# Attention and gated MLP in one kernel: pair 2's queries in the mixed order, bias rows ahead of V, w_in behind a cast, and a new order of slots 4 and 7 to 9

## The chip, the cores and the metric

The kernel runs on one core of one Trainium2 chip. The metric is the device time of one execution in microseconds. The kernel before took 354.9 us, the median of three runs (354.85, 354.90 and 356.21); the profiled execution has a span of 352.8 us. TensorE's granted clock was 1.00 throughout.

## What is computed

Batch 8, 8 heads, 576 positions, head dimension 64; then an MLP on 4608 tokens of width 512 with 2048 hidden units. All inputs are float32.

```python
scores = 0.125 * q @ k.T                         # per batch and head, 576 x 576
cum    = cumsum(maximum(s, 0))                   # per batch and head
scores = where(key > query, -1e9, scores + minimum(-(cum_query - cum_key), 0))
x      = softmax(scores) @ v                     # heads side by side: 4608 x 512
h      = x @ w_in                                # 4608 x 2048
out    = (h * clip(h + 3, 0, 6) / 6) @ w_out     # 4608 x 512
```

## The kernel before

**Tiling.** Heads are taken two at a time: 32 pairs, four to a batch. The main loop `for p in range(NP)` has one slot for each pair. Scores are held with keys on partitions and queries along the row. A head has three groups of scores (`scores(p, hh, g)`, L400 and L415), each in one bank of PSUM; ScalarE takes exp into `P` (L434). The last 64 keys and queries of both heads are the corner (`corner(p)`, L472 and L480). `av` multiplies P by V (L499), V carrying a column of ones whose product is the softmax sum; `norm` divides by it on VectorE (L521, L522); `transpose_x` turns x on TensorE (L536) and copies it to `xT` (L541). The MLP works on blocks of 512 tokens: `m1` makes one 128-wide strip of h (L565), with ScalarE's `tr` (L580) and VectorE's `gT` (L581) behind it; `m2` makes a quarter of the sum for an output tile (L592). `m1_begin` starts an m1 with those of its four terms that are there.

**The bias.** The sum of s is an addition to the scores, and it comes in through four extra rows of the q and k operands: partitions 64 to 67 of the tile `qk`, which DMA copies from `rows_of` (`load_aug(p)`, L169). `rows_of` is computed once for 32 heads in the first microseconds.

**Queries in two orders.** q and k are loaded as f16 with several positions in a partition's row, and TensorE transposes them (L278; L265 for the mixed order). A copy from PSUM then brings positions in place. In the plain order it writes every sixth and second element (L322). In the mixed order, which `mixed(p, i)` chooses for the queries of pairs 3 to 6, 64 queries stand in groups of 16, and the copy writes runs of 16 (L310). A mixed pair uses a permuted causal mask (`shutm`), permuted bias rows (row 0 of `rows_of`, made on GpSimd by the cast at L850), and a permutation instead of the identity in `transpose_x`.

**Masks.** Pairs 0 to 3 add the mask of the diagonal with a matmul (L389, L459); from pair 4 GpSimd sets the masked part of P to zero after exp (`shut_out`, L444), and `av` waits for that.

**Order of the work.** Every engine runs its instructions in the order in which the program records them[...]. GpSimd issues the loads of q, k, w_in (1 MB at a time) and w_out, casts V from f32 (`cast_v`, L218 and L219) and cuts P. SyncE issues the loads of V (`load_v`, three transfers to a pair, two raw buffers in turn), most bias rows and the output. Each of the two queues has eight completion semaphores in turn, so an issue also waits for the transfer eight issues before it. Which half of the MLP a `group()` call records is written out in `plan`, one character a call: 1 an m1, 2 an m2, a point nothing. In PSUM, scores have two banks from slot 4 on, `ph` two, `po` two, the transposed q or k one (`t`), so every one of them waits for the reader of the bank's last contents.

**Around the change.** Until slot 3 the MLP has nothing to do. Slot 4 (`p == PPB`) is the first with m1. Its part before:

```python
            m1_begin(0, 0, NKC - 1)
            scores(p, 0, 1)
            transpose_x(p - 1)
            scores(p, 0, 2)
            m1_begin(0, 1, NKC - 1)
            pt = transpose_in(p + 1, 0)
            transpose_out(p + 1, 0, pt, pars=(0,))
            group()
            transpose_out(p + 1, 0, pt, pars=(1,))
            group()
```

There the two query copies stand between the groups, one ahead of each. Slots 6 to 9 have the same split.

Of the kernel before, what the change touches and what calls it, by code (L numbers as in the profile page):

```python
# [18 lines left out]
def kernel(  # L19
# [97 lines left out]
    def load_qk(p, i):  # L117
        b, h0 = p // PPB, 2 * (p % PPB)
        src = (q, k)[i][b, h0 : h0 + 2]
        if not flat(p):  # L120
            if not i:
                tok = work.tile([128, 24 * D], F16, tag="tok", bufs=4, name="tok")
                toks[p] = tok[0:96].rearrange("p (i h e d) -> p i h e d", i=2, h=2, e=6)
            if mixed(p, i):
                nc.gpsimd.dma_start(
                    out=toks[p][:, i]
                    .rearrange("p h e d -> p (h e d)")
                    .rearrange("p (t x) -> p t x", t=3),
                    in_=src.rearrange("h s d -> (h s) d").rearrange(
                        "(t p e) d -> p t (e d)", p=96, e=4  # L130
                    ),
                )
                return
            nc.gpsimd.dma_start(
                out=toks[p][:, i].rearrange("p h e d -> p h (e d)"),
                in_=src.rearrange("h (p e) d -> p h (e d)", e=6),
            )
        else:
            if p < NSW:
                if not i:  # L140
                    tok = work.tile([128, 24 * D], F16, tag="tok", bufs=4, name="tok")
                    toks[p] = tok[:, 0 : 18 * D]
                to, eng = toks[p], nc.gpsimd
            else:
                to, eng = raws[p % NRAW], nc.sync
            eng.dma_start(
                out=to.rearrange("p (i t d) -> p i t d", i=2, t=9)[:, i],
                in_=src.rearrange("h s d -> (h s) d").rearrange(
                    "(t p) d -> p t d", p=128
                ),  # L150
            )

    def load_v(p, eng):
        b, h0 = p // PPB, 2 * (p % PPB)
        vraw = vraws[p % NVRAW]
        for hh in range(2):
            eng.dma_start(
                out=vraw[:, hh, 0:4, :],
                in_=v[b, h0 + hh, 0:512, :].rearrange("(t p) d -> p t d", p=128),
            )  # L160
        eng.dma_start(
            out=vraw[0:64, :, 4, :],
            in_=v[b, h0 : h0 + 2, 512:SEQ, :].rearrange("h p d -> p h d"),
        )

    def load_aug(p, eng):
        for hh in range(2):
            g = 2 * p + hh
            eng.dma_start(  # L169
                out=qks[p % NQK][64:68, hh, :, 64 * hh : 64 * hh + SEQ],  # L170
                in_=rows_of[g // 32].rearrange("(r g) i t -> g r i t", g=32)[
                    g % 32, :, slice(0, 3, 2) if mixed(p, 0) else slice(1, 3), 0:SEQ
                ],
            )
# [6 lines left out]
    def load_w_in(c):  # L181
        nc.gpsimd.dma_start(
            out=w_in_sb[:, :, 512 * c : 512 * (c + 1)],
            in_=moe_w_in[:, 512 * c : 512 * (c + 1)].rearrange(
                "(kc p) f -> p kc f", p=128
            ),
        )
# [28 lines left out]
    def cast_v(p):  # L216
        vraw, va = vraws[p % NVRAW], vas[p % NVA]
        nc.gpsimd.tensor_copy(out=va[:, :, 0:4, 0:64], in_=vraw[:, :, 0:4, :])  # L218
        nc.gpsimd.tensor_copy(out=va[0:64, :, 4, 0:64], in_=vraw[0:64, :, 4, :])  # L219
# [63 lines left out]
        return pt  # L283

    def mixed(p, i):
        return i == 0 and PPB - 1 <= p < NPROD - 1

    def mix(ap):
        return ap.rearrange("p (g w v) -> p g w v", w=4, v=16)

    def unmix(ap):
        return ap.rearrange("p (g v w) -> p g w v", w=4, v=16)
# [292 lines left out]
    def m2(n, i):  # L585
# [31 lines left out]
    tail = [False]  # L617
    LAG = 12
    plan = list(
        "11.1.1."  # L620
        + "1.1.1.1."
        + "1.1.1.1."
        + "1.1.1212"
# [212 lines left out]
    head_out(0, 0, 1, pts[0], (A, V.tensor_copy))  # L836
    head_out(0, 1, 1, pts[1], (V.tensor_copy, V.tensor_copy))
    warm(NWARM[2])
    load_aug(1, nc.gpsimd)
    load_v(1, nc.sync)  # L840
    load_aug(2, nc.sync)
    load_stair(PPB, nc.sync)
    cast_v(0)
    for i in range(2):
        load_qk(3, i)
    load_v(2, nc.sync)
    cast_v(1)
    for i in range(2):
        load_qk(4, i)
    nc.gpsimd.tensor_copy(  # L850
        out=mix(rows_of[0][0:32, 0, 0:SEQ]), in_=unmix(C["c"][0:32])
    )


    I, U = load_w_in, load_w_out
# [1 line left out]
    for p in range(NP):  # L857
# [7 lines left out]
                    load_qk(p + 3, i)  # L865

        if p == 2:
            load_w_in(0)
            cast_v(2)
            qk_ahead()  # L870
            load_aug(5, nc.gpsimd)
        elif p == 3:
            cast_v(3)
            qk_ahead()
            load_aug(6, nc.gpsimd)
            load_w_in(1)
            cast_v(4)
        elif p >= PPB:
            qk_ahead()
            if NPE <= p + 2 < NP:  # L880
                if p + 2 >= NSW:
                    cast_qk(p + 2)
                crossbar_qk(p + 2)
# [25 lines left out]
        if p and p + 2 < NP:  # L909
            load_v(p + 2, nc.sync)  # L910
        if p == 1:
            load_aug(3, nc.sync)
            load_aug(4, nc.sync)
        if p == 2:
            for i in range(PPB + 1, NPROD):
# [15 lines left out]
        def get(i):  # L931
            if p + 1 < NPE:
                transpose(p + 1, i)
            elif nxt:
                spread(p + 1, i)
# [22 lines left out]
        if p == PPB:  # L958
            early[0] = False
            scores(p, 0, 0)  # L960
            pool_mid()
            av(p - 1, 1, 0)
            av(p - 1, 1, 1)
            norm(p - 1, 1)
            m1_begin(0, 0, NKC - 1)
            scores(p, 0, 1)
            transpose_x(p - 1)
            scores(p, 0, 2)
            m1_begin(0, 1, NKC - 1)
            pt = transpose_in(p + 1, 0)  # L970
            transpose_out(p + 1, 0, pt, pars=(0,))
            group()
            transpose_out(p + 1, 0, pt, pars=(1,))
            group()
        else:
            scores(p, 0, 0)
            pool_mid()
            if NPROD - 1 <= p + 1 < NPE:
                pt = transpose_in(p + 1, 0)
                transpose_out(p + 1, 0, pt, pars=(0,))  # L980
                group()
                transpose_out(p + 1, 0, pt, pars=(1,))
            else:
                get(0)
                group()
            scores(p, 0, 1)
            av(p - 1, 1, 0)
            if p >= NPE - 1:
                get(1)
            group()  # L990
            scores(p, 0, 2)
            av(p - 1, 1, 1)
            norm(p - 1, 1)
            group()
        if p == 12:
            cum2(whole)
        corner(p)
        if p == 11:
            new_sum()
            cum1(1, whole)  # L1000
# [1 line left out]
        if p > NPE:  # L1002
            x_done[0] = p - 1
        if p == PPB:
            get(1)
            av(p, 0, 0)
        scores(p, 1, 0)
        pool_end()
# [5 lines left out]
        scores(p, 1, 1)  # L1014
        if p != PPB:
            av(p, 0, 0)
        if PPB < p < NPROD:
            transpose_x(p - 1)
        elif p >= NPROD and p != 3 * PPB:
            crossbar_x(p - 1)  # L1020
# [53 lines left out]
```

## Time and profile before

| | busy us | share of span | instructions |
|---|---|---|---|
| TensorE matmul | 344.1 | 98% | 2914 |
| VectorE | 230.5 | 65% | 476 |
| ScalarE | 222.0 | 63% | 395 |
| GpSimd | 166.6 | 47% | 296 |

Busy shares are means over the whole span. By stages (busy us of TensorE, VectorE, ScalarE and GpSimd in each stretch, and what DMA moved):

| stretch, us | TensorE | VectorE | ScalarE | GpSimd | GB/s |
|---|---|---|---|---|---|
| 0 to 20 | 17.57 | 17.25 | 15.60 | 18.54 | 164 |
| 20 to 35 | 13.32 | 11.41 | 12.74 | 9.66 | 196 |
| 35 to 50 | 15.00 | 14.06 | 13.39 | 14.68 | 197 |
| 50 to 65 | 14.42 | 10.77 | 10.33 | 10.12 | 192 |
| 120 to 160 | 40.00 | 27.10 | 27.88 | 23.79 | 183 |
| 300 to 353 | 49.15 | 21.92 | 16.08 | 0.00 | 50 |

A share near the length of the stretch means that the engine hardly rests there. The end of a matmul in the records is modelled, and the next may start before it, so time lost on TensorE is best read from the distances between starts. Slots 0 to 3 end at about 26 us, slot 4 lasts from 26.1 to 34.7, slots 5, 6 and 7 begin at 34.7, 41.3 and 48.0.

### The profile page before, as it was taken

Reading aid. Unit: us, or ns where it says so; the run is one execution under the profiler, and the core shown is the slowest. Engines: PE = TensorE matmul, PEld = TensorE weight load, DVE = VectorE, ACT = ScalarE, POOL = GpSimd, SP = SyncE. Lnnn points to the kernel's source line nnn. Section 1 sums busy time; section 2 is a strip of 40 time slices with the busy share of each in tenths; the row PEclk is TensorE's granted clock in tenths of the full one; section 3 lists DMA queues with packets and bytes.
Section 4 is the critical chain, followed back from the end, with each engine's and each line's share of the span. In section 5 each row is a group of like instructions: output and inputs, shape, how many; then the busy total and the mean of one; then the engine's idle time right before and its main releaser. Section 6 shows DMA issues by size and latency. Waiting matters only on the chain.

```text
span 352.8 us, 7771 instructions
## 1 busy us (share of the span) xinstructions
PE 344.1 (98%) x2914; PEld 190.8 (54%) x2914; DVE 230.5 (65%) x476; ACT 222.0 (63%) x395; POOL 166.6 (47%) x296
## 2 busy tenths in 40 slices
PE   8998999999999999999999999999999999999995
PEld 3775666655555555555555555555555444444442
DVE  7996996686868677666666665767654544544531
ACT  6987895677787677666766666666665333444410
POOL 8976995676778556555555555555310000000000
PEclk9999999999999999999999999999999999999999
DMA  8999999999999999889898969796120101101112
GB/s 162 155 201 192 194 200 197 148 201 177 159 124 124 211 204 178 180 187 175 185 168 191 179 156 196 164 207 140 37 74 20 59 17 46 59 2 59 59 39 82
DMA packets 144616, 48.59 MB, mean 138 GB/s; under 512 B 130537, under 2 KB 139593, under 8 KB 144578
## 3 DMA queue, kind: packets, MB, share of 16 engines
q1 hardware_dynamic: 117138, 37.83, 53.4%
q0 software_dynamic: 27200, 9.97, 23.9%
q8 instruction: 23, 0.38, 0.5%
q10 hardware_dynamic: 240, 0.28, 0.2%
q14 instruction: 15, 0.12, 0.1%
HBM read 37.59 MB, written 9.44 MB: 133 GB/s over the span
## 4 chain that ended last, share of the span: by engine, by line
PE 85%; DMA 5%; DVE 5%; ACT 3%; issue 1%; POOL 0%; SPq 0%; ACTq 0%
PE po L592 34%; PE ph L565 32%; PE O L499 7%; PE S L415 6%; PE S L400 3%; DMA vraw<-in_v_dram 3%; DMA tok<-in_k_dram 1%; DVE qk L242 1%; DVE gT L581 1%; DVE qk L322 1%; PE pt L278 1%; ACT P L434 1%; ACT tr L580 1%; DMA s_all<-in_s_dram 1%; DVE x L522 1%
## 5 line engine op out<-in xcount | busy, mean ns | idle before, releaser
L581 DVE SCALAR_TENSOR_TENSOR gT<-tr,ph 128x512 f16<-128x512 f32 x144 | 98.7, 686 | 98.5 <-ACT tr L580 97.4
L565 PE MATMUL ph<-xT,w_in_sb 128*128 128x512 f16 x576 | 148.0, 378 | 0.8 <-DVE gT L581 0.6
L592 PE MATMUL po<-w_out_sb,gT 128*128 128x512 f16 x576 | 145.8, 379 | 0.0
L580 ACT ACTIVATE tr<-ph,bias 128x512 f32<-128x512 f32 x144 | 98.9, 687 | 73.3 <-PE ph L565 71.3
L434 ACT ACTIVATE P<-S 128x512 f16<-128x512 f32 x192 | 111.4, 595 | 39.4 <-PE S L400 22.3
L565 PEld LDWEIGHTS <-w_in_sb 128*128 128x128 f16 x576 | 51.3, 97 | 45.3 <-issue 1.1
L592 PEld LDWEIGHTS <-gT 128*128 128x128 f16 x576 | 50.1, 97 | 46.5 <-issue 0.2
L444 POOL TENSOR_SCALAR_AFFINE_SELECT P<-P 128x512 f16<-128x512 f16 x56 | 37.8, 674 | 46.9 <-ACT P L434 46.8
L415 PE MATMUL S<-qk 68*128 68x448 f16 (+3 forms) x256 | 49.0, 272 | 0.6 <-ACT P L434 0.6
L499 PE MATMUL O<-va,P 128*128 128x65 f16 x896 | 47.7, 193 | 0.0
L499 PEld LDWEIGHTS <-P 128*128 128x128 f16 x896 | 39.2, 97 | 13.5
L242 DVE COPY qk<-jt 64x768 f16<-64x768 f16 x84 | 37.4, 446 | 1.2
L415 PEld LDWEIGHTS <-qk 68*128 68x128 f16 x256 | 23.7, 98 | 24.2 <-issue 0.7
L522 DVE TENSOR_TENSOR x<-O,rl 128x320 f16<-128x320 f32 x64 | 31.4, 491 | 2.2
L169 POOL DMA_DIRECT2D qk<-rows_of x50 | 29.8, 598 | 2.2 <-PE S L400 1.6
L608 DVE TENSOR_SCALAR ob<-po 128x512 f32<-128x512 f32 (+1 forms) x36 | 24.3, 676 | 8.3 <-PE po L592 7.7
L444 POOL TENSOR_SCALAR_AFFINE_SELECT PC<-PC 128x128 f16<-128x128 f16 x28 | 8.5, 304 | 43.0 <-ACT PC L480 42.9
L400 PEld LDWEIGHTS <-qk 75*128 75x128 f16 (+1 forms) x256 | 18.8, 97 | 12.9 <-DVE qk L322 1.4
L400 PE MATMUL S<-qk 75*128 75x128 f16 (+1 forms) x256 | 24.8, 219 | 0.9 <-DVE qk L322 0.6
L218 POOL CAST va<-vraw 128x512 f16<-128x512 f32 x32 | 21.1, 659 | 2.8 <-DMA vraw<-in_v_dram 2.8
L322 DVE COPY qk<-pt 64x576 f16<-64x576 f16 x22 | 17.6, 805 | 4.6 <-ACT qk L322 4.1
L214 POOL CAST tok<-raw 128x576 f16<-128x576 f32 x28 | 18.0, 681 | 0.0
(77 smaller groups left out, 188.0 us busy)
## 6 DMA issues: line engine op xcount, KB each, us to landing
out_dram<-ob SPq DMA_DIRECT2D x35, 256.0 KB, 2.0
vraw<-in_v_dram SPq DMA_DIRECT2D x64, 128.0 KB, 4.7
raw<-in_q_dram SPq DMA_DIRECT2D x14, 288.0 KB, 3.6
raw<-in_k_dram SPq DMA_DIRECT2D x14, 288.0 KB, 4.2
tok<-in_q_dram POOLq DMA_DIRECT2D x18, 144.0 KB, 5.3
tok<-in_k_dram POOLq DMA_DIRECT2D x18, 144.0 KB, 6.5
w_in_sb<-in_moe_w_in_dram POOLq DMA_DIRECT2D x4, 512.0 KB, 7.3
w_out_sb<-in_moe_w_out_dram POOLq DMA_DIRECT2D x8, 256.0 KB, 9.1
```

The costliest lines, as they stand in the source:

```text
L169: eng.dma_start(out=qks[p % NQK][64:68, hh, :, 64 * hh : 64 * hh + SEQ], in_=rows_of[g // 32].rearrange("(r g) i t -> g r i t", g=32)[g % ...
L242: copies[par](out=qk[0:64, :, i, 128 * par : 128 * par + 256 * n].rearrange("p h (s two c) -> p h s two c", two=2, c=128)[:, :, :, 0, :], ...
L400: mm(S[:, c], lhsT=kT[rows, c], rhs=qT[rows, c], start=(j == 0 and not by_product), stop=(j == 3 and p >= NROW),)
L415: mm(S[:, c : c + w], lhsT=kT[0:68, 128 * j : 128 * (j + 1)], rhs=qT[0:68, 128 * (j + 1) : SEQ], start=(c == 0), stop=(c != 0 and p >= NROW),)
L434: nc.scalar.activation(out=pt[:, c], in_=S, func=AF.Exp, scale=0.125)
L444: nc.gpsimd.affine_select(out=part, in_=part, pattern=pattern, compare_op=ALU.is_ge, fill=0.0, base=0, channel_multiplier=-1,)
L499: mm(o[:, i, :], lhsT=lhsT, rhs=va[:, hh, j, 0:65], **kw)
L522: nc.vector.tensor_tensor(out=X[p][:, :, hh, :], in0=o[:, :, 0:64], in1=rl.to_broadcast([128, 5, 64]), op=ALU.mult,)
L565: mm(ph, lhsT=w_in_sb[:, kc, ft * 128 : (ft + 1) * 128], rhs=xT[:, kc, n * 512 : (n + 1) * 512], start=(kc == 0), stop=(kc == NKC - 1),)
L580: nc.scalar.activation(out=tr, in_=ph, func=AF.Relu, bias=bias3[:, 0:1])
L581: nc.vector.scalar_tensor_tensor(out=gTs[n][:, ft, :], in0=tr, scalar=6.0, in1=ph, op0=ALU.min, op1=ALU.mult)
L592: mm(po, lhsT=gTs[n][:, ft, t4 * 128 : (t4 + 1) * 128], rhs=w_out_sb[:, ft, :], start=(ft == 0), stop=(ft == NFT - 1),)
```

## The change

Four edits. The third pair's queries (pair 2) are mixed too, so that their copies write runs. The bias rows of pairs 1, 2 and 3 are issued on SyncE, those of pairs 2 and 3 ahead of pair 3's V, and the permuting cast on GpSimd, on which pair 2's rows now depend, comes earlier; the loads of pair 3's q and k go ahead of the first cast of V. The first load of w_in goes behind the cast of pair 2's V. In slot 4 the corner and both copies of the next queries come right behind the transposed x, ahead of the second `m1_begin`, the keys (`get(1)`) move behind the second head's second scores, and `plan` moves one m1 accordingly. In slots 7 to 9 the query copies are no longer split around `group()`; in slot 6 they still are. In the order of TensorE both programs have the same 5830 rows.

```diff
--- before.py
+++ after.py
@@ -283,7 +283,7 @@
         return pt
 
     def mixed(p, i):
-        return i == 0 and PPB - 1 <= p < NPROD - 1
+        return i == 0 and PPB - 2 <= p < NPROD - 1
 
     def mix(ap):
         return ap.rearrange("p (g w v) -> p g w v", w=4, v=16)
@@ -617,7 +617,7 @@
     tail = [False]
     LAG = 12
     plan = list(
-        "11.1.1."
+        "11..11."
         + "1.1.1.1."
         + "1.1.1.1."
         + "1.1.1212"
@@ -836,20 +836,21 @@
     head_out(0, 0, 1, pts[0], (A, V.tensor_copy))
     head_out(0, 1, 1, pts[1], (V.tensor_copy, V.tensor_copy))
     warm(NWARM[2])
-    load_aug(1, nc.gpsimd)
     load_v(1, nc.sync)
-    load_aug(2, nc.sync)
+    load_aug(1, nc.sync)
     load_stair(PPB, nc.sync)
-    cast_v(0)
     for i in range(2):
         load_qk(3, i)
+    cast_v(0)
     load_v(2, nc.sync)
+    nc.gpsimd.tensor_copy(
+        out=mix(rows_of[0][0:32, 0, 0:SEQ]), in_=unmix(C["c"][0:32])
+    )
+    load_aug(2, nc.sync)
+    load_aug(3, nc.sync)
     cast_v(1)
     for i in range(2):
         load_qk(4, i)
-    nc.gpsimd.tensor_copy(
-        out=mix(rows_of[0][0:32, 0, 0:SEQ]), in_=unmix(C["c"][0:32])
-    )
 
 
     I, U = load_w_in, load_w_out
@@ -865,8 +866,8 @@
                     load_qk(p + 3, i)
 
         if p == 2:
+            cast_v(2)
             load_w_in(0)
-            cast_v(2)
             qk_ahead()
             load_aug(5, nc.gpsimd)
         elif p == 3:
@@ -909,7 +910,6 @@
         if p and p + 2 < NP:
             load_v(p + 2, nc.sync)
         if p == 1:
-            load_aug(3, nc.sync)
             load_aug(4, nc.sync)
         if p == 2:
             for i in range(PPB + 1, NPROD):
@@ -966,16 +966,15 @@
             scores(p, 0, 1)
             transpose_x(p - 1)
             scores(p, 0, 2)
+            corner(p)
+            get(0)
             m1_begin(0, 1, NKC - 1)
-            pt = transpose_in(p + 1, 0)
-            transpose_out(p + 1, 0, pt, pars=(0,))
             group()
-            transpose_out(p + 1, 0, pt, pars=(1,))
             group()
         else:
             scores(p, 0, 0)
             pool_mid()
-            if NPROD - 1 <= p + 1 < NPE:
+            if p + 1 == NPROD - 1:
                 pt = transpose_in(p + 1, 0)
                 transpose_out(p + 1, 0, pt, pars=(0,))
                 group()
@@ -994,7 +993,8 @@
             group()
         if p == 12:
             cum2(whole)
-        corner(p)
+        if p != PPB:
+            corner(p)
         if p == 11:
             new_sum()
             cum1(1, whole)
@@ -1002,7 +1002,6 @@
         if p > NPE:
             x_done[0] = p - 1
         if p == PPB:
-            get(1)
             av(p, 0, 0)
         scores(p, 1, 0)
         pool_end()
@@ -1014,6 +1013,8 @@
         scores(p, 1, 1)
         if p != PPB:
             av(p, 0, 0)
+        else:
+            get(1)
         if PPB < p < NPROD:
             transpose_x(p - 1)
         elif p >= NPROD and p != 3 * PPB:
```

## The prediction

> **What bounds the kernel now.** I read the page first (busy shares, slices), then TensorE's instructions in order of time, then those of VectorE and GpSimd, then the chain that ended last, in the early window alone. Columns of the instruction views: start, duration, engine and line, operation, shape, count, and in brackets the engine's idle time before it and what ended it.
>
> ```profile
> PE 344.1 (98%) x2914; PEld 190.8 (54%) x2914; DVE 230.5 (65%) x476; ACT 222.0 (63%) x395; POOL 166.6 (47%) x296
> ```
>
> TensorE sets the end. Only time in which it waits can be saved, since the change leaves its matmul count alone (5830 rows in the order of both programs). So I look for its waits:
>
> ```profile
> 16.38 0.38 PE L415 MATMUL S<-qk 68*128 68x320 f16 x2
> 17.16 0.45 PE L536 MATMUL ptx<-ident,x 128*128 128x128 f16 x5 [0.40 <-DVE x L522]
> ...
> 18.35 0.40 PE L400 MATMUL S<-qk 68*128 68x128 f16 x4 [0.22 <-DVE qk L322]
> ...
> 26.13 0.40 PE L400 MATMUL S<-qk 75*128 75x128 f16 x4 [0.41 <-DVE qk L322]
> ...
> 31.17 1.02 PE L565 MATMUL ph<-xT,w_in_sb 128*128 128x512 f16 x4 [0.59 <-DVE gT L581]
> ...
> 33.00 0.38 PE L415 MATMUL S<-qk 68*128 68x320 f16 x2 [0.59 <-ACT P L434]
> ...
> 34.56 0.20 PE L499 MATMUL O<-va,PC 128*128 128x65 f16 x1
> ...
> 52.23 0.42 PE L278 MATMUL pt<-ident,tok 96*128 96x96 f16 x6 [0.58 <-DVE qk L322]
> ```
>
> The bracket counts from a modelled end. By starts the waits are longer: the pair of L415 in front starts at 16.38 and needs 0.22 (two L415 starts elsewhere are 0.22 apart), so L536 could start at 16.60 and waits 0.56; likewise 0.4, 0.6, 0.75, 0.75, 0.2 and 0.75. Together some 4 us between 12 and 54 us, and hardly any later. That is the ceiling of this change: about 1.1% of 354.9.
>
> Next, who holds the wait at 34.56: the corner's P, cut on GpSimd (L444).
>
> ```profile
> 28.84 0.61 POOL L218 CAST va<-vraw 128x512 f16<-128x512 f32 x1 [2.47 <-DMA vraw<-in_v_dram]
> 29.40 0.29 POOL L219 CAST va<-vraw 64x128 f16<-64x128 f32 x1
> 29.64 0.66 POOL L134 DMA_DIRECT2D tok<-in_q_dram  x1
> 30.30 0.64 POOL L134 DMA_DIRECT2D tok<-in_k_dram  x1
> 30.93 0.91 POOL L444 TENSOR_SCALAR_AFFINE_SELECT P<-P 128x512 f16<-128x512 f16 x1
> 31.76 0.64 POOL L218 CAST va<-vraw 128x512 f16<-128x512 f32 x1
> 32.89 0.29 POOL L219 CAST va<-vraw 64x128 f16<-64x128 f32 x1 [0.49 <-DMA vraw<-in_v_dram]
> 33.36 0.77 POOL L182 DMA_DIRECT2D w_in_sb<-in_moe_w_in_dram  x1 [0.18 <-issue]
> 34.14 0.37 POOL L444 TENSOR_SCALAR_AFFINE_SELECT PC<-PC 128x128 f16<-128x128 f16 x1
> ```
>
> The chain in this window names what GpSimd waited for: one V transfer of 9.62 us.
>
> ```profile
> 19.16 9.62 DMA vraw<-in_v_dram
> 28.79 0.06 issue
> 28.84 0.61 POOL va L218
> ```
>
> **What the Trainium skill says.** *VectorE: DVE Perf Modes*, "What auto-detection actually checks": the two-at-a-time mode needs 16-bit elements with step 1. The trace agrees: L322 writes 576 elements at steps of 2 and 6 in 805 ns, L310 writes as many in runs of 16 in 450 ns. *DMA: Bandwidth & Descriptors*, "Issuing engines are not separate DMA queues" and "Queues, rings and completion order": transfers of all queues share 16 engines that take turns between queues, and a transfer is complete when its last engine is. The trace agrees as far as it goes: from 12 to 54 us 193 GB/s move, and V takes 9.62 us beside w_in. So moving an issue by 2 us doesn't move a landing by 2 us.
>
> **Part 1, third pair's queries mixed (`mixed` from pair 2).** Two L322 copies (14.70 to 16.35) become two L310: 2 x (805 - 450) = 0.71 us less on VectorE. It works without a gap from 14.70 to 18.3, and TensorE waits for it at 17.16 and 18.35. The half-head copy on ScalarE ending at 16.33 holds the next VectorE copy by under 0.1. So pair 2's first scores come at 17.65 instead of 18.35: **0.7 us** (0.5 to 0.7). Six transposes L265 cost what six L278 cost (205 against 206 ns); mask and permutation operands exchange tiles of equal size. Later waits of slots 2 and 3 (26.13) are VectorE's own chain and merely shift.
>
> **Part 2, loads and casts.** Bias rows of pair 1 go from GpSimd to SyncE: two issues, 1.2 us less on GpSimd, and the permuting cast L850 (1.25 us) comes earlier, so casts of V stay where they were within 0.2. Pair 2's bias rows now need that cast, which ends near 12.5 instead of being done at 16.06. SyncE issues them after V of pair 2, at 12.9 to 14.2, and they are needed at 17.6; hidden. In front of V of pair 3 stand four bias-row issues (four took 16.08 to 18.63, 2.55), so this V is issued at 15.5 to 17.2 instead of 13.38 to 15.13: **2.1 us later**. V of pair 4 follows at 18.3, as before. Queries of pair 3 are issued 2.3 earlier, at 9.1, into a stretch where DMA moved less (106 to 137 GB/s at 9 to 13.5 us, against 193 on the mean from 12 to 54). w_in stands behind the cast of pair 2's V, at about 16, as before, since L850 has left that place. New wait: this cast (needs V of pair 2, issued by 12.95; used at 16.77 without a wait before); behind it stand w_in and pair 5's loads, which have 10 us.
> Pair 3's V must be cast by 23.9, when TensorE now wants `av(3,0,0)` (24.59 less 0.7). The kernel before had it 5.2 us after its last issue (15.13 to 20.35). 17.2 + 5.2 = 22.4, cast 0.6: 23.0. No stall, by 0.9. High end: as slow as pair 4's V, 9.6 after its second issue at 16.0: 25.6, a stall of 2.3.
> Pair 4's V: equal traffic in front, but pair 6's q and k and pair 5's V come some 2 us later, and earlier loads filled the slack. Bounds 26.5 and 28.8; I take **27.8**.
>
> **Part 3, slot 4 (corner and queries behind x).** Scores of (4,0,2) are followed at once by the corner, whose bank ScalarE must first empty of (4,0,1). Before, ScalarE ended that 1.1 us after these scores started; so the corner adds a wait near **0.3** on TensorE, with queries, m1 and everything else queued behind. The chain m1(0,0), tr, gT, m1(0,2) (29.29, 29.71, 30.43, 31.17) then starts at 28.9, 0.4 earlier instead of 0.7. Behind m1(0,2) the wait of 0.75 at 33.00 vanishes: scores (4,1,1) now stand ahead of m1, and ScalarE has no key copy between tr and P. TensorE could reach the corner's product at 33.1 (34.56 less the 0.2 of its own wait, 0.75, 0.4, and 0.2 for scores (4,1,1), which now lie inside m1's wait: 33.0; I take 33.1). There GpSimd rules. From V's landing to the end of the corner's cut: casts 0.85, two issues 1.3, cut 0.83, casts 0.85, issue 0.77, cut 0.37, sum 5.0 without waits; 27.8 + 5.0 = 32.8. Before, 28.84 + 5.0 = 33.8 became 34.5 through waits, mostly for the tail of pair 5's V, which here is issued later or no earlier; I keep all of that 0.7: 33.5. So **1.0 us** is won by the end of slot 4, part 1 included (0.2 if V lands as before, 1.45 if GpSimd falls behind TensorE).
>
> **Part 4, slots 7 to 9: both copies ahead of `group()`.** At 52.23 TensorE waits for the bank emptied at 52.17. Both copies now run from 49.98 to 51.6: 0.6 less. But gT, ahead of the second copy before (50.67), ends near 52.3 now, and m1 at 52.48 needs its bank: so **0.15** is left (0 to 0.6). In slots 8 and 9 neither m1 nor a wait stands there; nothing.
> Sum: 1.0 + 0.15 = 1.15; 354.9 - 1.15 = 353.75, so **353.7**. Behind slot 7 TensorE hardly waits, so a gain stays, as long as w_out (last landing 63.2, first use 63.4 to 63.9) moves too; GpSimd's earlier w_in issue fills a dip of DMA at 34 to 36 us.
>
> **Rivals.**
> - *GpSimd unmoved, no change to speak of.* Pair 4's V still lands at 28.8, as bandwidth, not issue time, sets it: slot 4 gives back the 0.7; gain 0.2 + 0.15, 354.5. For it: saturated DMA. Against: later loads behind this V.
> - *All waits go.* Slot 4 at 33.1 or earlier and the full 0.6 in slot 7: 1.5 + 0.6 = 2.1, 352.8. For it: 4 us of waits exist. Against: the corner's new wait, VectorE 36.7 of 42 us busy.
> - *Pair 3's V late, slower.* Landing 25.6, stall 2.3, less 0.7; it delays pair 6's loads and pair 5's V, so GpSimd's cut comes near 35.5: 34.56 becomes 35.6, less 0.15: 355.8. For it: V beside w_in took 9.6. Against: pair 3's V took 5.2 with w_in beside it too.
>
> **How the numbers follow.** Forecast 0.40, GpSimd unmoved 0.27, all waits gone 0.20, late V 0.13. The range takes in most of both outer cases: 352.6 to 355.8. Faster by over 0.5% (under 353.1): nearly all of the third case and a twentieth of the first, 0.25. Slower (over 356.7): only the bad half of the late V, 0.08. Within: 0.67.
>
> **What would show it.** Pair 2's scores L400 near 17.65; a wait of TensorE at the corner L472 near 27.7; V cast L218 of pair 3 before 23.5 and of pair 4 near 27.8; corner cut ending near 33.5; L278 near 51 with m1 waiting for gT after it. Wrong if `av(3,0,0)` waits for V, if pair 2's bias rows land after 17.6, or if gT's later place starts a row of waits in slots 8 and 9.

## The result and the profile after

The changed kernel takes **357.88 us** (median of 4 runs, 357.5 to 358.13) against 355.39 (4 runs, 354.85 to 356.21): a ratio of **1.0067, 95% interval [1.0041, 1.0093]**, 2.5 us slower. A second series gave 357.75, ratio 1.0066 [1.0026, 1.0107]. The forecast was 353.7 (352.6 to 355.8). In what follows the ratios and the counts of runs by clock leave out disturbed runs (over 1.5% above the fastest of the same kernel), which the medians contain, so where they differ the ratio decides.

The page of the changed kernel, busy shares and the clock granted to TensorE in 40 slices of 8.9 us:

```profile
PE 345.1 (97%) x2914; PEld 191.3 (54%) x2914; DVE 230.0 (65%) x476; ACT 221.7 (62%) x395; POOL 165.2 (46%) x294
...
PEclk9999899999999999999999999999999999999999
```

TensorE has as many instructions as before and 1.0 us more work, although nothing was added to it. The fifth slice (36 to 45 us) shows why: there the clock fell. Everything lost was lost near it. By the start of one and the same instruction in both traces, the changed kernel is 0.5 us ahead at the start of slot 4 (25.64 against 26.13), 1.95 behind at the start of slot 5 (36.61 against 34.66) and 3.3 behind at that slot's second head (41.25 against 37.91); from there the distance only moves between 3.3 and 3.6.

TensorE's instructions in order of time (start, duration, line, operation, shape, count; in brackets its idle time before and what ended it by the record):

```profile
17.86 0.40 PE L400 MATMUL S<-qk 68*128 68x128 f16 x4
...
28.11 0.22 PE L472 MATMUL Sc<-qk 75*128 75x64 f16 x2
...
32.89 0.44 PE L499 MATMUL O<-va,P 128*128 128x65 f16 x9
...
36.51 0.20 PE L499 MATMUL O<-va,PC 128*128 128x65 f16 x1 [3.18 <-DMA tok<-in_k_dram]
36.61 0.38 PE L400 MATMUL S<-qk 75*128 75x128 f16 x4
...
39.44 1.90 PE L565 MATMUL ph<-xT,w_in_sb 128*128 128x512 f16 x4
...
41.25 0.54 PE L400 MATMUL S<-qk 75*128 75x128 f16 x4
...
55.12 0.41 PE L278 MATMUL pt<-ident,tok 96*128 96x96 f16 x6
55.84 1.02 PE L565 MATMUL ph<-xT,w_in_sb 128*128 128x512 f16 x4 [0.30 <-DVE gT L581]
```

The same two starts of slot 5, first and second head, in the kernel before:

```profile
34.66 0.38 PE L400 MATMUL S<-qk 75*128 75x128 f16 x4
...
37.91 0.38 PE L400 MATMUL S<-qk 75*128 75x128 f16 x4
```

Two things to read. Ahead of the product with the corner's P TensorE stands **3.2 us** idle (3.3 by the starts, as in the tables below). The transfer that the bracket names isn't its reason: the product needs the corner's cut, and that ends at 36.45 (below); in the second series' trace the bracket of the same wait names the cut. And after it four matmuls of 512 columns last 1.90 us where elsewhere four last 1.02: their starts lie 411 to 427 ns apart instead of 213. That is **half the clock**, and the first half of slot 5 takes 4.64 us instead of 3.25.

GpSimd, which makes that cut:

```profile
17.22 0.61 POOL L218 CAST va<-vraw 128x512 f16<-128x512 f32 x1 [2.79 <-DMA vraw<-in_v_dram]
...
18.01 0.79 POOL L182 DMA_DIRECT2D w_in_sb<-in_moe_w_in_dram  x1
...
29.15 0.61 POOL L218 CAST va<-vraw 128x512 f16<-128x512 f32 x1 [2.10 <-DMA vraw<-in_v_dram]
...
34.84 0.29 POOL L219 CAST va<-vraw 64x128 f16<-64x128 f32 x1 [1.96 <-DMA vraw<-in_v_dram]
35.31 0.76 POOL L182 DMA_DIRECT2D w_in_sb<-in_moe_w_in_dram  x1 [0.18 <-issue]
36.09 0.36 POOL L444 TENSOR_SCALAR_AFFINE_SELECT PC<-PC 128x128 f16<-128x128 f16 x1
```

The same two instructions in the kernel before, in their old order:

```profile
15.99 0.79 POOL L182 DMA_DIRECT2D w_in_sb<-in_moe_w_in_dram  x1
16.77 0.62 POOL L218 CAST va<-vraw 128x512 f16<-128x512 f32 x1
```

The first line of the changed kernel is the cast of pair 2's V, now ahead of w_in(0), the first load of w_in: it waits 2.79 us, and w_in(0) is requested at 18.01 instead of 15.99. At 34.84 the tail of pair 5's V comes late, and behind it in GpSimd's order stand a request and the cut: the cut ends 1.95 us later than before.

What DMA did meanwhile, first the changed kernel and then the one before (window, length, busy time of each engine with its count, clock, DMA share, GB/s):

```profile
17.00:20.00 3.00, 2.85 (x57) 2.30 (x55) 2.86 (x7) 2.64 (x8) 2.78 (x5) 1.00 0.52 99
...
17.00:24.00 7.00, 6.81 (x127) 5.55 (x125) 6.40 (x16) 6.64 (x16) 6.78 (x12) 1.00 0.88 145
```

```profile
17.00:20.00 3.00, 2.62 (x52) 2.19 (x53) 2.91 (x8) 1.99 (x5) 3.00 (x6) 1.00 1.28 207
...
17.00:24.00 7.00, 6.58 (x123) 5.46 (x124) 6.45 (x16) 5.99 (x13) 5.79 (x11) 1.00 1.26 203
```

From 17 to 20 us the engines of DMA stood half empty while GpSimd held w_in(0) back. (203 - 145) GB/s for 7 us is 0.41 MB, 2.0 us of the rate before. Since the changed kernel had moved more from 7 to 17 us (168 GB/s against 156, 0.12 MB), about 0.29 MB are missing at 24 us, or **1.4 us**. That is one execution, and the emptiest: in four other traces with the same loads up to slot 4 (the second series, and d, g and c below) 159 to 191 GB/s moved from 17 to 24 us.

### The profile page after: what moved, and what is told of

The parts are those of the page before. It is cut to its first block, busy times and chain, and to the rows that moved or that the text cites. A ratio compares the mean times of both kernels' runs of the same rounds, so it can differ in the third digit from the quotient of the medians.

```text
span 356.4 us, 7772 instructions
## 1 busy us (share of the span) xinstructions
PE 345.1 (97%) x2914; PEld 191.3 (54%) x2914; DVE 230.0 (65%) x476; ACT 221.7 (62%) x395; POOL 165.2 (46%) x294
## 4 chain that ended last, share of the span: by engine, by line
PE 83%; DVE 6%; DMA 5%; ACT 3%; issue 1%; POOL 0%; ACTq 0%; SPq 0%; POOLq 0%
PE po L592 34%; PE ph L565 31%; PE O L499 7%; PE S L415 6%; PE S L400 3%; DMA vraw<-in_v_dram 2%; DMA tok<-in_k_dram 2%; DVE gT L581 2%; DVE qk L322 1%; DVE qk L242 1%; ACT P L434 1%; ACT tr L580 1%; DMA s_all<-in_s_dram 1%; DVE x L522 1%; DVE qk L344 1%
## 5 line engine op out<-in xcount | busy, mean ns | idle before, releaser
L592 PE MATMUL po<-w_out_sb,gT 128*128 128x512 f16 x576 | 145.8, 379 | 0.0
L592 PEld LDWEIGHTS <-gT 128*128 128x128 f16 x576 | 50.1, 97 | 46.5 <-issue 0.2
L169 POOL DMA_DIRECT2D qk<-rows_of x48 | 28.5, 596 | 0.6 <-POOL rows_of L783 0.3
L400 PE MATMUL S<-qk 75*128 75x128 f16 (+1 forms) x256 | 25.0, 220 | 0.8 <-DVE qk L322 0.4
L400 PEld LDWEIGHTS <-qk 75*128 75x128 f16 (+1 forms) x256 | 18.8, 98 | 12.9 <-DVE qk L322 1.3
L322 DVE COPY qk<-pt 64x576 f16<-64x576 f16 x20 | 16.0, 804 | 5.0 <-ACT qk L322 4.8
```

What stands on the lines that cost most here:

```text
L169: eng.dma_start(out=qks[p % NQK][64:68, hh, :, 64 * hh : 64 * hh + SEQ], in_=rows_of[g // 32].rearrange("(r g) i t -> g r i t", g=32)[g % ...
L400: mm(S[:, c], lhsT=kT[rows, c], rhs=qT[rows, c], start=(j == 0 and not by_product), stop=(j == 3 and p >= NROW),)
L592: mm(po, lhsT=gTs[n][:, ft, t4 * 128 : (t4 + 1) * 128], rhs=w_out_sb[:, ft, :], start=(ft == 0), stop=(ft == NFT - 1),)
```

## Experiments

Theory **H**: w_in(0) behind the waiting cast leaves DMA empty and shifts all later loads, and with them V and the corner's cut. Theory **C** adds that a good part of the loss is the clock that falls after the stall. The rival of H is that some other part costs: the mixed queries, the bias rows ahead of V, or the new order of the slots. Each kernel ran beside the kernel before, and is called by the first letter of its name.

### The parts: slots alone, loads alone

The kernel before with the new slots 4 and 7 to 9 and nothing else (f_slots_only), and the changed kernel with the slots as before, so the loads together with the mixed queries (g_loads_only).

> The kernel before with parts 3 and 4 alone (slot 4 with corner and query copies behind x, queries of slots 7 to 9 not split); queries of pair 2 and all loads as before. If the loss lies in the loads: GpSimd ends the corner's cut near 34.5 as before, TensorE comes there earlier and waits longer, slot 7 gains 0.1: the time is 354.5 to 355.5. If the order of the slots loses by itself: above 356.

> The changed kernel without parts 3 and 4: pair 2's queries mixed, the new order of loads and casts, w_in behind the cast; slot 4 and 7 to 9 as before. If the loss lies in the loads: the corner's cut ends near 36.4, TensorE waits there for 1.5 to 2.5 us, with a dip of the clock after it, and the time is 356.5 to 358. If the slot order is what loses: 354 to 355.

Slots alone: 355.28, ratio 0.9995 [0.9974, 1.0016]. Loads and mixed queries: 358.08, ratio 1.0057 [1.0005, 1.0109], with TensorE idle 1.5 us at the same product and the clock at 0.72 after it. So **the loss lies in the loads and the mixed order that they serve**; the slots by themselves cost nothing that shows. They do win on the way: the m1 behind L278 in slot 7 starts at 51.74 instead of 52.48. Where that 0.74 goes is taken up below.

### w_in's place and the bias rows' place

```
         if p == 2:
-            cast_v(2)
             load_w_in(0)
+            cast_v(2)
```

This edit in the changed kernel is a_win_first; its reverse in the kernel before is b_win_behind. l_rows_behind puts only pair 3's bias rows back:

```
     load_aug(2, nc.sync)
-    load_aug(3, nc.sync)
     cast_v(1)
...
         if p == 1:
+            load_aug(3, nc.sync)
             load_aug(4, nc.sync)
```

e_v3_first and e_again (the same kernel twice) do both.

> The changed kernel with w_in's first load back ahead of the cast of pair 2's V; nothing else differs. Theory H (w_in held): in the changed kernel GpSimd stood 2.79 us at that cast (until 17.22), w_in was issued at 18.0 instead of 16.0, DMA was nearly empty from 17 to 20 us, and all later loads, the tail of pair 5's V last, came 2 us later. Then w_in is issued near 14.4, the corner's cut ends 2 us earlier or more (34.4 at the latest instead of 36.45), and the time is 353.5 to 354.5. Theory R (bias rows ahead of V): the four bias-row issues on SyncE, not w_in, make V of pairs 3, 4 and 5 late. Then the cut still ends after 35.5 and the time stays above 356.5.

> The kernel before with one exchange: the cast of pair 2's V ahead of w_in's first load. Theory H: w_in is issued near 17 (cast 16.06 to 17.0, V's tail landed at 16.7) instead of 16.0, so loads behind it come up to 1 us later and the corner's wait grows: 355.5 to 357. Theory R: w_in's place is of no account: within 0.3% of before.

> The changed kernel with only pair 3's bias rows put back behind pair 3's V; w_in(0) still stands behind the cast of pair 2's V. Theory H (the cast holds w_in back, all later loads follow): the cut of the corner still ends after 35.5, the stall of TensorE there stays above 1.5 us, time 357 to 358. Rival R (the bias rows ahead of V are what delays V of pairs 4 and 5): the stall goes below 1 us and the time falls to 355 to 356.

> The changed kernel with w_in ahead of the cast again and, beside that, pair 3's bias rows issued behind pair 3's V, as in the kernel before; pair 2's stay ahead. With w_in first alone, pair 3's V was issued at 15.5 to 17.6 behind w_in (14.5), landed at 26 and held TensorE for 2.8 us. Theory R (bias rows ahead of V are the loss, w_in behind the cast only hides it): V is now issued at about 14.2, lands by 21.5, that wait goes, and the time is 353.5 to 355. Theory H2 (w_in must not come before V, whoever is ahead): V still lands after 24, and the time is above 356.5.

> The changed kernel with w_in(0) ahead of the cast of pair 2's V and pair 3's bias rows behind its V, once more for its trace. If the two load edits are the whole loss (theory H), the time is near that of the kernel before with slots reordered, 354.0 to 355.3, and the cut of the corner ends by 34.5. If the loss also lies in what stays changed ahead of them (q and k of pair 3 and the bias rows of pairs 1 and 2 moved in the queue), 356 to 357, and some V or the cut still comes over 1 us later than before.

| kernel | w_in(0) requested | median us | ratio, interval | where TensorE stalls |
|---|---|---|---|---|
| changed | 18.0 | 357.88 | 1.0067 [1.0041, 1.0093] | 3.3 at the corner's product |
| l: rows back | 17.2 | 358.42 | 1.0078 [1.0042, 1.0114] | 2.8 there |
| a: w_in back | 14.5 | 357.62 | 1.0059 [1.0034, 1.0084] | 2.8 at pair 3's V |
| e: both back | 14.5 | 356.33, 356.69 | 1.0023 [1.0001, 1.0046], 1.0025 [0.9996, 1.0054] | 3.1 at pair 3's bias rows, 0.8 at the corner |
| b: before, w_in behind | 17.5 | 355.86 | 1.0025 [0.9997, 1.0053] | 1.8 at the corner's product |

In l the stall stays with the bias rows put back, which speaks for H and against the rival; in b the swap alone makes such a stall, though its time is not clearly apart from the kernel before. But **a refutes H in the form I had**: w_in(0) is back in its place and nothing is won. GpSimd and TensorE in a:

```profile
26.24 0.60 POOL L218 CAST va<-vraw 128x512 f16<-128x512 f32 x1 [5.59 <-DMA qk<-stairm]
```

```profile
26.90 0.43 PE L499 MATMUL O<-va,P 128*128 128x65 f16 x5 [2.66 <-POOL va L218]
```

This is pair 3's V, cast at 26.24 instead of 21.30, the late V of my third rival. Its reason is that w_in(0) comes *earlier than before*: the permuting copy of 1.25 us that held it until 15.99 has moved away, so it is requested at 14.51, ahead of pair 3's V (15.47 to 18.58). With the rows behind V as well, the next in line suffers (e, second series; the trace of the first is of an odd execution of 1274 us, see the end):

```profile
24.48 0.38 PE L400 MATMUL S<-qk 68*128 68x128 f16 x4 [2.95 <-DMA qk<-rows_of]
```

So the changed kernel and a are two sides of one thing: w_in(0), 1 MB of f32 that lands as 512 KB of f16, on the DMA engines that also bring V and bias rows with a date. At 14.5 it goes ahead of them, at 18.0 it leaves DMA empty first.

### The mixed order alone

The kernel before with only pair 2 mixed, and the least that needs: the permuting copy right behind `load_aug(1)`, pair 2's bias rows behind its V. k_mixed_slots adds the new slots.

> The kernel before with only the third pair's queries in the mixed order, and the least that this needs: the permuting copy of the constant rows right behind load_aug(1) on GpSimd, and the third pair's bias rows behind its V; casts, w_in and slots as before. If the mixed order is worth what the transposes show (0.5 us at the third pair's scores) and the loads are the whole loss, 354.3 to 355.2. If the mixed order itself costs (later casts behind the permuting copy), 355.5 to 356.5.

> The same with the changed slots 4 and 7 to 9 as well, so everything of the change but the new order of the loads. If the loads are the whole loss, 353.8 to 354.9, ahead of both kernels; if the reordered slots need the earlier loads, 355.5 or more.

A miss: 357.34, ratio 1.0064 [1.0041, 1.0087], and 356.87, ratio 1.0054 [1.0025, 1.0083]. The copy stands ahead of the first casts, which come 1.2 us later (11.79 instead of 10.59); pair 2's V waits for its buffer and is requested at 12.44 instead of 11.24, its bias rows follow at 14.12 to 15.41, pair 3's V at 15.52, its bias rows at 17.27, behind w_in(0) at 15.99. TensorE waits for those rows again:

```profile
24.38 0.38 PE L400 MATMUL S<-qk 68*128 68x128 f16 x4 [2.80 <-DMA qk<-rows_of]
```

In j and k **the mixed order has a price in the loads**: a copy of 1.25 us that must come early, and bias rows that no longer fit into SyncE's idle time ahead of pair 2's V.

### Restoring the sequence

p_rows2_pool puts pair 2's bias rows on GpSimd right behind the copy, so that SyncE can request pair 3's V behind pair 2's and pair 3's rows behind that, with w_in(0) ahead of the cast; q_rows2_behind is the same with w_in(0) behind.

```
     )
-    load_aug(2, nc.sync)
-    load_aug(3, nc.sync)
+    load_aug(2, nc.gpsimd)
     cast_v(1)
...
```

> The changed kernel with the loads in the sequence that the kernel before had as far as the mixed order allows: pair 2's bias rows on GpSimd's queue right behind the permuting copy, so that SyncE requests pair 3's V right behind pair 2's, pair 3's bias rows behind that V, w_in(0) ahead of the cast. If the order of requests is the whole loss: pair 3's V and bias rows are requested by 16 and 17.5, w_in(0) at 15.6, no stall above 1 us before 36, time 353.6 to 354.8, below both kernels. If something else of the change costs: 355.5 or more.

> The same with w_in(0) behind the cast of pair 2's V as in the changed kernel. If the cast's wait alone holds w_in(0) and all behind it back: w_in(0) at 17 or later, a stall of 1 to 3 us at the cut of the corner, 0.5 to 2.5 us above the kernel with w_in(0) ahead. If no wait for the cast is left with these loads: the same time as that kernel within 0.5 us.

p missed: ratio 1.0047 [1.0023, 1.0072]. Pair 3's V was requested at 14.6, its rows at 16.7, w_in(0) at 16.1, much as I wanted, and yet TensorE waited 0.7 for the rows at 23.0, 1.1 for pair 4's V and 2.8 at the corner. q: 1.0071 [1.0038, 1.0104]; w_in(0) at 17.6, the stall 2.9. The two intervals overlap, so the pair says nothing certain on the cast's wait by itself. The order of these three requests is not the whole of it.

### DMA's idle time, and the order of GpSimd at the corner

m_qk_first lets other loads fill the gap behind the waiting cast; c_cut_first puts the corner's cut ahead of the cast of pair 5's V; h_v3_cut does that to e; r_qk_cut joins m and c.

```
         if p == 2:
+            qk_ahead()
             cast_v(2)
             load_w_in(0)
-            qk_ahead()
```

```
...
             corner(p)
+            shut_out(p, PCs[p % 2][:, 0:128], 64)
+            pool_mid()
             get(0)
...
```

> The changed kernel with q and k of pair 5 requested ahead of the cast of pair 2's V instead of behind w_in(0); w_in(0) still stands behind the cast. The loads that sit idle behind the waiting cast can then fill the empty DMA of 17 to 20 us. Theory H (the DMA time lost there is the loss): 17 to 20 us above 150 GB/s, cut of the corner by 35, time 354.5 to 356. Theory W (it is the place of w_in(0) itself against V, whatever fills the gap): pair 3's V or the cut late by over 1.5 us again, 357 to 358.

> The changed kernel with GpSimd's cut of slot 4's corner ahead of the cast of pair 5's V and of w_in's third load, so that the wait of 3.4 us at the corner's product no longer hangs on V's tail. Loads are as in the changed kernel. If that wait is the whole loss: the wait goes, the cast of pair 5's V (ends 35.1 in the changed kernel) then holds TensorE for 0 to 1 us in slot 5, the granted clock has no dip, and the time is 353 to 354.5. If the late loads cost elsewhere too (w_in's second megabyte, pair 5's V), the stall moves to slot 5 and the time is 355.5 or more.

> As the kernel with w_in first and pair 3's V ahead of pair 3's bias rows, and the corner's cut of slot 4 ahead of the cast of pair 5's V. If theory R holds and the cut's place saves what GpSimd still holds TensorE for: 353.0 to 354.3, faster than both kernels. If pair 5's V or w_in's megabytes hold slot 5 anyway: within 0.3 us of the same kernel without the cut's move.

> The changed kernel with q and k of pair 5 ahead of the cast of pair 2's V and with the corner's cut ahead of the cast of pair 5's V. If the idle DMA and GpSimd's order were the whole loss, no stall above 1 us up to 50 and 354 to 355, ahead of the kernel before. If the loads as a whole set a floor (the last w_out landed at 63.2 before and at 65.5 with q and k first), what is won by 50 is given back at w_out near 61 to 66, and the time is 355.3 to 356.7.

| kernel | DMA 17 to 24 us, GB/s | corner's product stalls | ratio, interval |
|---|---|---|---|
| changed | 145 | 3.3 | 1.0067 [1.0041, 1.0093] |
| m | 197 | 1.65 | 1.0039 [1.0010, 1.0068] |
| c | 191 | none; 0.9 for w_in(1), 0.9 at slot 5's corner | 1.0046 [1.0014, 1.0077] |
| r | 202 | none | **1.0007 [0.9982, 1.0031]** |

h, whose trace is of such an odd execution too: 1.0040 [1.0017, 1.0062]. The 191 of c is not its edit's work, which begins in slot 4: up to there its loads are those of the changed kernel, which moved 145, 167, 159 and 181 in the other four traces with them. With q and k first it was 190 to 202 in three (m, r, t), 203 to 206 with the loads of the kernel before (before, f). So q and k first do fill the gap, but the gap's size in the changed kernel varies from run to run. m shows what H expected in its trace, 159 GB/s from 17 to 20 us and the cut's end at 34.8, but not in its time: its median is 357.7, since its runs fall into two groups (below). Each mend alone stays clear of the kernel before; **both together bring the time back to that of the kernel before**. The interval of r overlaps those of m and c, so what each mend adds to the other isn't measured. The cut in r:

```profile
30.63 0.38 POOL L444 TENSOR_SCALAR_AFFINE_SELECT PC<-PC 128x128 f16<-128x128 f16 x1
30.93 0.64 POOL L218 CAST va<-vraw 128x512 f16<-128x512 f32 x1
32.79 0.29 POOL L219 CAST va<-vraw 64x128 f16<-64x128 f32 x1 [1.23 <-DMA vraw<-in_v_dram]
```

The tail of V is still waited for, but the cut no longer stands behind it. And now the gain of the change can be followed to where it ends. In r TensorE is well ahead in slot 7, and then waits for w_out twice:

```profile
51.52 1.02 PE L565 MATMUL ph<-xT,w_in_sb 128*128 128x512 f16 x4 [0.30 <-DVE gT L581]
...
60.45 0.59 PE L592 MATMUL po<-w_out_sb,gT 128*128 128x512 f16 x2 [0.53 <-DMA w_out_sb<-in_moe_w_out_dram]
...
64.26 0.59 PE L592 MATMUL po<-w_out_sb,gT 128*128 128x512 f16 x2 [0.54 <-DMA w_out_sb<-in_moe_w_out_dram]
65.17 1.03 PE L592 MATMUL po<-w_out_sb,gT 128*128 128x512 f16 x4
```

| | m1 of slot 7 starts | last w_out landed | L592 behind it starts |
|---|---|---|---|
| before | 52.48 | 63.18 | 64.75 |
| f (slots) | 51.74 | 63.58 | 64.53 |
| r (both mends) | 51.52 | 64.22 | 65.17 |

A lead of 0.74 in f becomes 0.22, one of 0.96 in r becomes a lag of 0.42. The last w_out is requested 11 to 12.5 us before it lands (before: 52.09, f: 51.46, r: 51.77), so it is not its request that is late: DMA moves 196 to 197 GB/s from 48 to 60 us in before, f and r alike. **The loads up to w_out are a floor** that TensorE reaches once it is ahead; in c, d, m and p it waits 0.8 to 1.1 us for w_out too. How hard the floor is stays untested: no run asks for w_out earlier, and in the same stretch the changed kernel, being late, moved 214 GB/s.

### The clock

d_filler adds 14 matmuls of 512 columns ahead of the stalled product (their result is thrown away; 3.0 us of work at full clock) to the changed kernel, t_qk_filler adds them to m. after_again is the changed kernel itself.

```
+        if p == PPB:
+            W = psum.tile([128, 512], F32, tag="po", bufs=2, name="W")
+            for _ in range(14):
+                mm(W, lhsT=xT[:, 0, 0:128], rhs=xT[:, 0, 0:512], start=True, stop=True)
         av(p, 0, 1)
```

> The changed kernel with 14 matmuls of 512 columns more (3.0 us of work whose result nobody reads) in slot 4 ahead of the product that waits for the corner's cut. Theory C (clock): the stall of 3.4 us made the chip grant a lower clock from 38.5 to 41.1 us, which cost 1.4 us on top. Then the filler hides in the stall, the clock stays at 1.00 and the time falls by 1.0 to 1.5 to about 356.6. If the dip has another cause: no change or up to 0.3 us slower.

> The changed kernel itself, once more, for how its runs spread: the kernel before showed a mean clock of 0.996 or less in 24 of 200 runs, at 358.1, and full clock in 176, at 355.1. If the change loses by stalling nearly always where the kernel before seldom does: 9 in 10 of its runs at a clock of 0.996 or less, 357.5 to 358.5 in all. If its four runs were a chance: half or more at full clock, median below 356.5.

> The changed kernel with q and k of pair 5 ahead of the cast, and 14 filler matmuls of 512 columns (their result is thrown away) ahead of the product that waits for the corner's cut. If the clock falls for want of matmuls in the stall, the filler keeps it at 1.00 in nearly all runs (against 9 of 17 that fell without it), and the median goes from 357.5 to 355.2 to 356.5. If the clock falls for another reason, half the runs still fall and the filler's 3 us add to the time: 357.5 or more.

d: 356.76, ratio 1.0048 [1.0026, 1.0070]: **with 3.0 us more work not slower, and by the medians 1.1 us faster**. By the ratios it is 0.7 us, and the intervals overlap, so the gain in time isn't certain. In d's trace the loads are as late as ever; only TensorE isn't idle:

```profile
32.99 3.19 PE L1034 MATMUL W<-xT 128*128 128x512 f16 x14
36.01 0.44 PE L499 MATMUL O<-va,P 128*128 128x65 f16 x9
36.70 0.20 PE L499 MATMUL O<-va,PC 128*128 128x65 f16 x1 [0.24 <-DMA vraw<-in_v_dram]
```

The product comes at 36.70 against 36.51 in the changed kernel, but the clock stays at 1.00 behind it, and the first half of slot 5 takes 3.26 us instead of 4.64: **1.4 us are the clock's**. t: 356.21, ratio 1.0029 [1.0012, 1.0047]. The mean clock of each run shows the same in bulk:

| kernel | runs at a mean clock of 0.996 or less, median | runs above, median |
|---|---|---|
| before | 28, 358.0 | 211, 355.15 |
| changed (both series) | 8, 357.9 | 1, 355.1 |
| changed + filler (d) | 2, 359.6 | 18, 356.7 |
| m | 9, 358.2 | 8, 355.4 |
| m + filler (t) | 1, 358.7 | 19, 356.2 |
| c | 0 | 12, 356.65 |
| r | 3, 357.4 | 17, 355.65 |
| f | 1, 357.7 | 18, 355.2 |

The kernel before has the low clock too, in 28 of 239 runs, and is then as slow as the changed one; the only run of the changed kernel at full clock is as fast as the kernel before. With the filler 2 of 20 runs have the low clock instead of 8 of 9. This speaks for a change that **does not so much add 2.5 us to every run as make a seldom stall the rule**; but it rests on that one run, and no low-clock run of the kernel before was traced. Nor do all kernels split like this: k's 14 low-clock runs (356.9) are no slower than its 2 others (357.1). The difference of the two columns (2.8 us in before) is stall and clock together.

## Why the prediction was wrong

- **Part 1 was right.** Pair 2's scores come at 17.86 (forecast 17.65; before 18.35), and 0.5 of the forecast 0.7 us stand at the start of slot 4.
- **Part 2 is the step that failed**: "w_in stands behind the cast of pair 2's V, at about 16, as before, since L850 has left that place", and "New wait: this cast ... behind it stand w_in and pair 5's loads, which have 10 us". I named the wait and gave it no size, because the cast had none before at 16.77. But GpSimd now reaches it at 14.4, and pair 2's V landed at 17.10. The wait measured 2.79, w_in(0) moved 2.0 later; in the four other traces with the same loads the wait was 1.15 to 2.05. It comes mostly of GpSimd's early arrival: V itself landed at 15.50 to 17.10 in these five traces and at 15.42, 16.45 and 17.13 in three that have the loads of before up to there (before, b, f). And it is not w_in's own date that mattered (it landed at 23.70, before at 24.08), but that DMA stood half empty from 17 to 20 us: the 10 us of slack belonged to w_in, not to the queue behind it. That this is what made the later V late is argued; what is shown is that r, which fills the gap and moves the cut, loses nothing that shows.
- **Pair 3's V** was no problem, as forecast: its cast starts at 21.30 (forecast: done by 23.0), though its first request comes 2.1 us later (15.44 against 13.38), as forecast. The rival in which it is late came true in a, where w_in(0) goes ahead of it.
- **Pair 4's V, 27.8**: it was cast at 29.15, beyond my bounds of 26.5 and 28.8 (before: 28.84). The gain of 1.0 that I gave it did not come.
- **Part 3.** The corner's own wait was 0.22 (forecast 0.3). "I keep all of that 0.7" of GpSimd's waits was mis-sized: the tail of pair 5's V alone took 1.96. SyncE requested it at 28.66 (before: 27.02), since that request takes over the completion semaphore of a pair 4 transfer that landed at 28.60. Fifteen of that transfer's sixteen shares had come by 26.80, little later than before (26.34, the last at 26.96), so it was one late share that held the request. I had it "issued later or no earlier" and still gave it no more time. From the start of pair 4's cast the cut needed the 5.0 of the forecast and 2.3 of waits: 29.15 + 7.3 = 36.45. Against the forecast of 33.5 that is 2.95 more, 1.35 for pair 4's V and 1.6 for the waits. Instead of 1.0 us won by the end of slot 4, 1.95 were lost.
- **The clock** was in no term of the sum: the first half of slot 5 took 1.4 us longer, in d, where the clock stays, it took 3.26 us (before: 3.25).
- **Part 4 was right**: L278 by itself waits no more, m1 stands 0.30 for gT, as forecast; from L400 to m1 it is 1.14 us instead of 1.22, so 0.08 are won where 0.15 was forecast. But "a gain stays, as long as w_out ... moves too" was the condition that fails: w_out doesn't move, and f and r give their lead back there. In f the loads' floor leaves 0.2 us of the lead.

The Trainium skill, in *DMA: Bandwidth & Descriptors* ("Queues, rings and completion order"), says that each DMA engine takes turns between the rings with work. I cited that page for "moving an issue by 2 us doesn't move a landing by 2 us", and drew from it only comfort. For q and k of pair 3, requested 2.3 us earlier, it held: they landed at 15.36 and 15.77 against 14.99 and 16.29. It cuts the other way too: an early request takes its turn from another with a nearer date, as w_in(0) took it from pair 3's V in a, whose second transfer, requested at 15.90, landed at 26.11 (the changed kernel: 16.26 and 19.61).

On the clock, *TensorE: Matmul & The Clock Gate* ("What's actually happening") says that TensorE's activity is watched in windows of 3413 ns that run freely, and that the clock is half after an idle window. The changed kernel's trace, in steps of 1 us (the last but two columns are the clock, 1.00 at full rate):

```profile
37.00:38.00 1.00, 1.00 (x11) 0.53 (x9) 0.99 (x3) 0.60 (x1) 1.00 (x3) 1.00 0.92 139
38.00:39.00 1.00, 1.00 (x13) 0.78 (x12) 0.43 (x2) 0.85 (x2) 0.99 (x2) 0.58 1.23 205
39.00:40.00 1.00, 1.00 (x13) 0.72 (x12) 0.86 (x3) 0.81 (x2) 1.00 (x3) 0.50 1.24 207
40.00:41.00 1.00, 1.00 (x4) 0.29 (x2) 0.38 (x1) 0.00 (x0) 1.00 (x3) 0.50 1.30 199
41.00:42.00 1.00, 1.00 (x14) 0.85 (x13) 0.00 (x0) 0.63 (x2) 1.00 (x2) 0.71 1.12 179
42.00:43.00 1.00, 1.00 (x9) 0.45 (x6) 0.69 (x1) 1.00 (x5) 0.89 (x3) 1.00 1.04 141
```

The missing shares, (0.42 + 0.50 + 0.50 + 0.29) x 2, make 3.42 us at half rate: one such window. Worked out the same way, b, g, k and l have 3.4 us and a and q 6.8, so lengths agree. That the windows run freely agrees too: behind the last matmul the clock falls once more, and in each of these traces the two falls lie a whole number of windows apart (38.16 and 355.60 in the changed kernel: 93 times 3.413; a: 97, b: 94). What doesn't agree is that the window must be idle: the one that ends where the clock falls, at 38.16, began at 34.75 and was idle only until 36.51, 1.8 of 3.4 us.

The last fall tells where the windows lie in a trace whose clock did not fall before, too. In the eight traces with a fall, TensorE is busy for 1.25 to 1.65 us of the window that ends there. In the four that stalled without a fall, the end of a window cuts the stall in two, and the two windows are busy for 1.89 and 1.99 us (e), 1.96 and 2.07 (j), 2.39 and 2.94 (m), 2.08 and 2.10 (p). So by these twelve traces **the clock falls when one window is idle for more than about half its length**, and a stall of 3 us can pass without harm where it spans two. The clock came back in all eight after a window of half rate without a gap; where a gap of 0.6 us (a) or 0.7 (q) was left in that window, it stayed at half for one more.

What stays open: why p, with the requests near the old sequence, still stalls; whether the splitting of m's runs is the windows' phase or the spread of V's landing, since both move by run; and what makes one of the sixteen shares of a transfer late (below), and whether the empty DMA has a part in it. The twelve traces with a stall of 1.5 us or more are the changed kernel twice, a, b, g, k, l and q, whose clock falls, and e, j, m and p, whose clock doesn't; no run moved a stall against the windows on purpose.

## What to carry to other kernels

Where DMA is full, ask of a moved request not when its own data are needed, but whether DMA runs empty while it is held back, and whom it overtakes when it comes early; a wait on an engine that also issues loads is paid by every load behind it. Put work that another engine needs now (here the cut) ahead of work on that queue that can wait for a load (here the cast of V). And before a gain of 1 us is put into the sum, look for the next landing downstream that TensorE would reach early, here w_out.

## What the runs showed that I had not expected

- Idle TensorE costs twice: after a stall of 1.5 to 3.8 us eight of twelve traces show the clock at half for 3.4 or 6.8 us. Where the stall lies against the windows decided it, and 14 useless matmuls in the stall took the low clock from 8 of 9 runs to 2 of 20.
- One late share of sixteen holds a transfer. Of pair 2's V in the changed kernel, 15 of the 16 increments of the three completion semaphores had come by 14.76, 15.14 and 15.32, the sixteenth at 16.25, 17.10 and 17.28. A packet of 16384 B of the instruction queue lies beside it, from 15.63 to 17.15; that it is the cause is only argued, and beside the late share of pair 4's V (26.80 and 28.60; second series 26.79 and 28.83) there is none. The kernel before has such shares too: of pair 4's second transfer 15 had come by 27.11, the sixteenth at 28.79.
- Of two loads requested 2.3 us earlier, one landed 0.4 us later than before and one 0.5 earlier.
- In one execution of e and one of h, matmuls of 512 columns followed each other at 840 ns, about four times the 213 elsewhere, for the whole program (1274 us), while the mean clock on record was 1.00; why is not known.
